# Attention and two feed-forward layers: both products of weights and v of a head pair become one operation, the last block of keys gets 128 rows, and the order of the operations is another

## The chip, the cores and the metric

The kernel runs on one core of a Trainium2 chip. The metric is the device time of one execution in microseconds. TensorE (PE) multiplies, VectorE (DVE), ScalarE (ACT) and GpSimd (POOL) do the elementwise work, and SyncE (SP) issues the DMAs.

## The reference, cut to what matters

```python
batch, n_heads, seq, head_dim = (4, 8, 576, 64)
scores = q @ k.T / sqrt(64)
mask = (pos[:, None] // 64) >= (pos[None, :] // 64)     # block-causal, blocks of 64
attn = softmax(where(mask, scores, -1e9))
x = (attn @ v) as [4 * 576 tokens, 512]
x = ((x @ w1) * (x @ w2)) @ w3 @ w_out                  # 512 -> 1024 -> 1024 -> 512
out = elu(x @ w_in) @ w_out2                            # 512 -> 2048 -> 512
```

## The kernel before

The 32 heads are handled as 16 head pairs, two heads of 64 columns side by side. One call of `attention(n, ...)` records the work of pair n: the scores of four groups of 128 queries (`group`, `first_groups`; L641, L648, L715) and of a last block of 64 queries (`last_block`; L780, L786), row maxima on VectorE, exponentials on ScalarE, transposes of the weights on TensorE (L687, L760, L820, L829) into PSUM tiles `t`, copies of them into the SBUF tiles `pt` (a helper at L518 on ScalarE or L519 on VectorE), and the products of weights and v (`pv`, L850) into PSUM tiles `o`, which the same helper copies into `xy`. The sums of the exponentials go out to memory, come back broadcast as `rr`, and `norm` multiplies `xy` by them.

Weights stand transposed in three tiles: `pts[0]` for queries 0 to 255, `pts[1]` for queries 256 to 575 and keys 0 to 511, and `pts[2]` for queries 512 to 575 and the last 64 keys. `pv(0)` multiplies `pts[0]` and v, `pv(1)` multiplies `pts[1]` and `pts[2]` and v. The two heads of a pair take the left and the right half of the array's columns (`o()[D * h:D * h + D, ...]`), so a matmul of L850 stands in the trace as a tile of 128*64, and the one over the last 64 keys as a tile of 64*64. An f32 matmul leaves two records there. All PSUM tiles `t` and `o` of attention take turns on two banks: `turn("to", (3, 4), ...)`.

Beside attention, TensorE has `w_product` (L928: w3 and w_out multiplied into one matrix, 128 records in f32 from the converted tiles `full`), then `block2` (L1042: a and b, L1003: y; 384 columns each) for six tiles of 384 tokens, and then the second feed-forward layer (`part_h`, L1293, and `part_o`, L1372). Weights come as 64-bit words into `cr` and are converted by ScalarE, VectorE and GpSimd before TensorE takes them (L422 to L458).

Nothing runs in the order in which it is written. Every `add` records an operation with its engine, a length and a priority, and `Plan.run` builds one list of them per engine: at each step it takes, of what is ready by its lengths, the one of lowest priority. `TURNS` replaces the priority of single operations by their number, and so sets the order by hand; a matmul of `spare` (L1594) is put in where the plan sees TensorE idle. An engine runs its list strictly in that order.

Of the kernel before, what the change touches and what calls it, by code (L numbers as in the profile page):

```python
# [20 lines left out]
P = 128  # L21
# [264 lines left out]
def attention_moe_moe2(  # L286
# [11 lines left out]
    nc = tc.nc  # L298
    B, NPAIR, _, S = qT.shape
    D = 64  # L300
# [222 lines left out]
    def attention(n, first_op):  # L523
# [36 lines left out]
        for j in range(2):  # L560
            add("SP", 0, lambda j=j: load_v(j), w=[(vt, j)], prio=pr + 2, nbytes=(P * 512 * 4, P * 64 * 4)[j])
# [275 lines left out]
        def pv(c, seq):  # L837
# [18 lines left out]
            if c:  # L856
                r += [(pt, "q"), pts[2], (vt, 1)]
# [794 lines left out]
```

## Time and profile before

| | us |
|---|---|
| median of 3 runs (895.3 to 899.37) | 895.55 |
| the profiled execution | 893.4 |
| span of its trace | 891.3 |
| TensorE busy, share of the span | 98% |
| VectorE, ScalarE, GpSimd busy | 80%, 57%, 61% |

The span runs from the first to the last instruction; the profiled execution is 2.1 us longer than it. Times below are from the span's start.

### The profile page before, as it was taken

What the parts mean: (1) busy time and instruction counts of PE and PEld (TensorE: products, weight loads), DVE (VectorE), ACT (ScalarE), POOL (GpSimd) and SP (SyncE); (2) the same over time, 40 slices, a digit from 0 to 9 for tenths busy, and PEclk for the clock granted to TensorE, in tenths of its full rate; (3) what the DMA queues carried; (4) which work ended last, traced back from release to release, by engine and by line L of the source; (5) the groups of instructions that cost most, each with busy time, mean ns of one, the idle gap of its engine ahead of it and who ended that gap; (6) DMA issues with size and microseconds to landing.
All of it is one profiled execution on the core that took longest, in us unless ns stands there. A gap on an engine that the chain in (4) does not pass through costs nothing.

```text
span 891.3 us, 15293 instructions
## 1 busy us (share of the span) xinstructions
PE 875.9 (98%) x5233; PEld 783.3 (88%) x5233; DVE 717.4 (80%) x1375; ACT 504.0 (57%) x1143; POOL 546.1 (61%) x552
## 2 busy tenths in 40 slices
PE   7999999999999999999999999999999999999998
PEld 4554488888788889999999999999999999999997
DVE  6998898888666666757888899888997779886886
ACT  7877678666655654326354554455644556454461
POOL 3677778654432315768878893136975268942695
PEclk9999999999999999999999999999999999999999
DMA  7867533555422106767585957777688766888656
GB/s 226 246 197 249 185 138 126 165 183 154 146 68 81 42 14 235 254 232 245 168 271 168 330 189 250 246 257 238 234 301 289 259 243 228 296 272 297 229 176 225
DMA packets 101037, 186.14 MB, mean 209 GB/s; under 512 B 8544, under 2 KB 51040, under 8 KB 100960
## 3 DMA queue, kind: packets, MB, share of 16 engines
q1 hardware_dynamic: 100960, 185.18, 63.0%
q8 instruction: 41, 0.67, 0.3%
q14 instruction: 36, 0.29, 0.1%
HBM read 147.85 MB, written 37.30 MB: 208 GB/s over the span
## 4 chain that ended last, share of the span: by engine, by line
PE 82%; DVE 7%; DMA 4%; ACT 2%; issue 2%; POOL 2%; SPq 1%; POOLq 0%; DVEq 0%; ACTq 0%
PE b L1042 10%; PE a L1042 10%; PE y L1003 10%; PE hx L1293 8%; PE ox L1372 8%; PE oz L1372 6%; PE hy L1293 5%; PE hz L1293 5%; PE oy L1372 5%; PE o L850 3%; PE wps L928 3%; PE t L687 2%; DMA cr<-w3T 2%; PE s L648 2%; DMA cr<-w 1%
## 5 line engine op out<-in xcount | busy, mean ns | idle before, releaser
L1003 PE MATMUL y<-g,slab_lo 128*128 128x384 f32 x576 | 115.6, 339 | 1.2 <-DVE xy L1026 1.0
L1042 PE MATMUL a<-xs,slab_lo 128*128 128x384 f32 x576 | 112.0, 337 | 0.0
L1042 PE MATMUL b<-xs,slab_lo 128*128 128x384 f32 x576 | 111.5, 337 | 0.3 <-DVE af L1059 0.3
L1003 PEld LDWEIGHTS y<-g,slab_lo 128*128 128x128 f32 x576 | 99.4, 188 | 3.8 <-DVE xy L1026 1.8
L1042 PEld LDWEIGHTS b<-xs,slab_lo 128*128 128x128 f32 x576 | 100.2, 188 | 0.6 <-DVE af L1059 0.6
L1042 PEld LDWEIGHTS a<-xs,slab_lo 128*128 128x128 f32 x576 | 100.1, 188 | 0.6 <-issue 0.5
L1293 PE MATMUL hx<-sy,win 128*128 128x384 f32 x432 | 86.4, 334 | 0.0
L1293 PEld LDWEIGHTS hx<-sy,win 128*128 128x128 f32 x432 | 75.8, 188 | 0.1
L1372 PE MATMUL ox<-sp,wout 128*128 128x384 f32 x372 | 74.6, 334 | 0.0
L964 POOL TENSOR_TENSOR g<-af,g 128x384 fp32r<-128x384 f32 x48 | 54.6, 1141 | 29.4 <-ACT g L961 27.2
L1372 PEld LDWEIGHTS ox<-sp,wout 128*128 128x128 f32 x372 | 65.4, 188 | 0.0
L928 PE MATMUL wps<-full,full 128*128 128x512 f32 x128 | 58.5, 597 | 2.9 <-POOL full L452 2.9
L1166 POOL TENSOR_TENSOR sp<-sum,sp 128x384 fp32r<-128x384 f32 x30 | 32.5, 1087 | 45.0 <-ACT sp L1165 45.0
L1293 PE MATMUL hz<-sy,win 128*128 128x384 f32 x288 | 57.9, 335 | 0.2
L1293 PE MATMUL hy<-sy,win 128*128 128x384 f32 x288 | 57.5, 334 | 0.0
L422 ACT ACTIVATE cr<-cr 128x512 int32<-128x512 uint32 x72 | 48.7, 680 | 12.4 <-DMA cr<-w 8.4
L449 POOL TENSOR_TENSOR ct<-ct,cr 128x512 int32<-128x512 int32 x28 | 39.9, 1431 | 22.5 <-DVE ct L443 14.8
L429 ACT ACTIVATE ct<-cr 128x512 f32<-128x512 f32 x58 | 39.4, 678 | 25.1 <-POOL wt L452 15.7
L850 PE MATMUL o<-pt,v 128*64 128x320 f32 (+4 forms) x448 | 52.7, 367 | 0.2
L1372 PE MATMUL oz<-sp,wout 128*128 128x384 f32 x264 | 52.0, 335 | 0.5 <-DVE cp L1175 0.5
L850 PEld LDWEIGHTS o<-pt,v 128*64 128x64 f32 (+1 forms) x448 | 27.8, 135 | 27.6 <-issue 5.5
L1372 PE MATMUL oy<-sp,wout 128*128 128x384 f32 x252 | 51.8, 334 | 0.0
(193 smaller groups left out, 2166.6 us busy)
## 6 DMA issues: line engine op xcount, KB each, us to landing
wout<-wso SPq DMA_DIRECT2D x84, 512.0 KB
cr<-w SPq DMA_DIRECT2D x48, 512.0 KB
win<-wsi SPq DMA_DIRECT2D x24, 1024.0 KB
win<-wsi SPq DMA_DIRECT2D x24, 768.0 KB
cr<-w3T SPq DMA_DIRECT2D x16, 512.0 KB
wsi<-wh SPq DMA_DIRECT2D x8, 896.0 KB
wsi<-wt SPq DMA_DIRECT2D x8, 896.0 KB
wso<-wh SPq DMA_DIRECT2D x8, 896.0 KB
```

Of the source, the lines that this page charges most:

```text
L422: nc.scalar.activation(out=low, in_=low.bitcast(U32), func=AF.Copy, scale=2.0**-29)
L429: nc.scalar.activation(out=t().bitcast(F32), in_=words()[1].bitcast(F32), func=AF.Abs)
L449: nc.gpsimd.tensor_tensor(out=t(), in0=t(), in1=words()[0], op=ALU.add)
L648: nc.tensor.matmul(sb[h]()[:, 0:w], lhsT=qs()[r, a, g * P:(g + 1) * P], rhs=ks()[r, c, 0:w], start=(x == 0), stop=(x == 2 and not added),)
L850: nc.tensor.matmul(o()[D * h:D * h + D, lo:cols], lhsT=vt()[0:kn, j, D * h:D * h + D], rhs=p, start=(j == 0), stop=(j == last),)
L928: nc.tensor.matmul(ps(), lhsT=a[:, j, :], rhs=bb, start=(j == 0), stop=(j == KF - 1))
L964: lambda: nc.gpsimd.tensor_tensor(out=g()[:, 1, :], in0=src(), in1=g()[:, 0, :].bitcast(F32), op=ALU.subtract),
L1003: nc.tensor.matmul(ps()[:, 0:T2], lhsT=w[:, a, n * P:(n + 1) * P], rhs=gs[m]()[:, c, :], start=(m == ms[0] and q == 0), stop=(m == ms[-1] ...
L1042: nc.tensor.matmul(ps()[:, 0:T2], lhsT=w[:, a, u, k, :], rhs=xs()[:, k, c, :], start=(k == 0 and q == 0), stop=(k == KD - 1 and q == 2),)
L1166: lo = lambda eng: eng.tensor_tensor(out=dst(1), in0=src(), in1=dst(0).bitcast(F32), op=ALU.subtract)
L1293: nc.tensor.matmul(bk()[:, 0:T3], lhsT=w[:, a, k, :], rhs=s_(c), start=(first and k == 0 and i == 0), stop=(k == 1 and i == 2), skip_group ...
L1372: nc.tensor.matmul(to[n]()[:, 0:T3], lhsT=w[:, a, n * P:(n + 1) * P], rhs=sp(c), start=(first and q == 0 and i == 0), stop=(q == KP - 1 an ...
```

## The change

`pv` is called once for each head pair, after `last_block`, and records one TensorE operation that multiplies first queries 0 to 255 (four matmuls, into one PSUM tile) and then queries 256 to 575 (ten, into the other); it takes both banks of the turn at once. The last block of keys is made 128 rows long: the transpose at L829 takes keys 448 to 575 and not 512 to 575, v has 64 rows of zeros put in at row 512 by the host, and v's second load takes 128 rows, 64 KB and not 32 KB. So the last two matmuls of a product are tiles of 128*64 like the others. The two copies out of PSUM stay two. `TURNS` is a new table, so the order of all engines is another one.

```diff
 TURNS = {
-    5: -2499.99, 16: -2329.56, 17: -2495.99, 29: -2498.01, 32: -2329.57, 33: -10133.18, 35: -2499.98, 41: -2499.99,
...
+    4: -2500.59, 5: -2499.99, 21: -2498.03, 24: -2399.95, 32: -2399.94, 42: -2500.01, 44: -2518.58, 46: -2499.94,
...
             if j:
-                nc.sync.dma_start(out=vt()[0:64, 4, :], in_=v[b, 512:576, hp * P:(hp + 1) * P])
+                nc.sync.dma_start(out=vt()[:, 4, :], in_=v[b, 512:640, hp * P:(hp + 1) * P])
...
             add(
-                "PE", 0.109, lambda: nc.tensor.transpose(t1()[0:D, 0:P], p()[:, 512:576], ident),
+                "PE", 0.109, lambda: nc.tensor.transpose(t1()[:, 0:P], p()[:, 448:576], ident),
                 r=[(p, 1), "ident"], w=[t1], prio=pg, kind="t",
             )
             evac(
-                128, lambda: pts[2]()[0:D], lambda: t1()[0:D, 0:P].rearrange("p (h q) -> p h q", h=2),
+                128, lambda: pts[2](), lambda: t1()[:, 0:P].rearrange("p (h q) -> p h q", h=2),
                 [t1], [pts[2]], pg,
             )
 
-        def pv(c, seq):
+        def pv(seq):
             pg = pr + 2 + seq
-            pt = pts[c]
-            o = turn("to", (3, 4), "o")
-            q0, cols = ((0, 256), (256, 320))[c]
-            last = (q0 + cols - 1) // P
+            os_ = [turn("to", (3, 4), "o") for _ in range(2)]
+            spans = ((0, 256), (256, 320))
 
             def product():
-                for j in range(last + 1):
-                    lo = max(0, j * P - q0)
-                    kn = min(P, S - j * P)
-                    for h in range(2):
-                        p = pts[2]()[0:kn, h, :] if j == 4 else pt()[:, h, j, lo:cols]
-                        nc.tensor.matmul(
-                            o()[D * h:D * h + D, lo:cols], lhsT=vt()[0:kn, j, D * h:D * h + D],
-                            rhs=p, start=(j == 0), stop=(j == last),
-                        )
-
-            r = [(pt, h, 2 * c + g) for h in range(2) for g in range(2)] + [(vt, 0)]
-            if c:
-                r += [(pt, "q"), pts[2], (vt, 1)]
-            add("PE", (0.8, 2.353)[c], product, r=r, w=[o], prio=pg, kind="pv")
+                for c, (q0, cols) in enumerate(spans):
+                    last = (q0 + cols - 1) // P
+                    for j in range(last + 1):
+                        lo = max(0, j * P - q0)
+                        for h in range(2):
+                            p = pts[2]()[:, h, :] if j == 4 else pts[c]()[:, h, j, lo:cols]
+                            nc.tensor.matmul(
+                                os_[c]()[D * h:D * h + D, lo:cols], lhsT=vt()[:, j, D * h:D * h + D],
+                                rhs=p, start=(j == 0), stop=(j == last),
+                            )
+
+            r = [(pts[g // 2], h, g) for h in range(2) for g in range(4)]
+            r += [(pts[1], "q"), pts[2], (vt, 0), (vt, 1)]
+            add("PE", 2.9, product, r=r, w=os_, prio=pg, kind="pv")
...
         group(2, 2)
-        pv(0, 2.5)
         group(3, 3)
         last_block(4)
-        pv(1, 5)
+        pv(5)
...
-        "vt": lay(v.transpose(0, 2, 1, 3)).reshape(B, S, H * D),
+        "vt": lay(np.insert(v.transpose(0, 2, 1, 3).reshape(B, S, H * D), [512] * 64, 0.0, axis=1)),
```

Two places on TensorE show how the order moves; lines of the changed kernel are a few numbers lower (L850 is L844 there, L829 is L824). The first is the start of the program. Before, the first product of the first head pair (pt_201) stands ahead of the second pair's first scores, and its second product (pt_256) some forty rows behind them:

```order
L687 MATMUL t_268<-ident,p_263 128x128 x4
L780 MATMUL s_275<-k_130,qw 128x288
L850 MATMUL o_284<-pt_201,v_180 64x256 x2
L850 MATMUL o_284<-pt_201,v_180 64x128 x2
L715 MATMUL s_300<-k_247,q_193 128x256
...
L928 MATMUL wps_354<-full_320,full_341 128x512
...
L829 MATMUL t_374<-ident,p_293 64x128
L760 MATMUL t_387<-ident,p_348 128x128
L760 MATMUL t_387<-ident,p_377 128x128
L850 MATMUL o_392<-pt_256,v_180 64x320 x6
L850 MATMUL o_392<-pt_256,v_180 64x192 x2
L850 MATMUL o_392<-pt_381,v_180 64x64 x2
```

In the changed kernel the same place reads:

```order
L775 MATMUL s_279<-k_130,qw 128x288
L682 MATMUL t_284<-ident,p_277 128x128 x4
...
L710 MATMUL s_305<-k_244,q_193 128x256
...
L815 MATMUL t_332<-ident,p_295 128x128 x4
...
L844 MATMUL o_351<-pt_201,v_180 64x256 x2
L844 MATMUL o_351<-pt_201,v_180 64x128 x2
L844 MATMUL o_356<-pt_254,v_180 64x320 x6
L844 MATMUL o_356<-pt_254,v_180 64x192 x2
L844 MATMUL o_356<-pt_341,v_180 64x64 x2
L643 MATMUL s_389<-k_244,q_193 128x384
```

Both products now stand behind the second pair's first scores and ahead of the first `wps` and of that pair's next scores.

The second place is a pair in the middle of attention (before: o_2799 and o_2917; s are scores, t transposes, a and b the block2 matmuls):

```order
L648 MATMUL s_2790<-k_2365,q_2291 128x512
L850 MATMUL o_2799<-pt_2746,v_2495 64x256 x2
L850 MATMUL o_2799<-pt_2746,v_2495 64x128 x2
L687 MATMUL t_2809<-ident,p_2770 128x128 x3
L1042 MATMUL b_2816<-xs_2190,slab_lo_1227 128x384 x12
...
L820 MATMUL t_2886<-ident,p_2873 128x128 x4
L829 MATMUL t_2893<-ident,p_2873 64x128
...
L715 MATMUL s_2897<-k_2607,q_2549 128x256
L850 MATMUL o_2917<-pt_2786,v_2495 64x320 x6
L850 MATMUL o_2917<-pt_2786,v_2495 64x192 x2
L850 MATMUL o_2917<-pt_2914,v_2495 64x64 x2
L648 MATMUL s_2956<-k_2607,q_2549 128x384
```

The same pair in the changed kernel:

```order
L643 MATMUL s_2790<-k_2358,q_2304 128x512
L682 MATMUL t_2801<-ident,p_2774 128x128 x3
L1038 MATMUL a_2808<-xs_2171,slab_lo_1236 128x384 x12
...
L815 MATMUL t_2911<-ident,p_2888 128x128 x4
L824 MATMUL t_2921<-ident,p_2888 128x128
...
L710 MATMUL s_2925<-k_2583,q_2529 128x256
L844 MATMUL o_2948<-pt_2753,v_2473 64x256 x2
L844 MATMUL o_2948<-pt_2753,v_2473 64x128 x2
L844 MATMUL o_2953<-pt_2786,v_2473 64x320 x6
L844 MATMUL o_2953<-pt_2786,v_2473 64x192 x2
L844 MATMUL o_2953<-pt_2941,v_2473 64x64 x2
L643 MATMUL s_2985<-k_2583,q_2529 128x384
```

The first product has left its place between scores and transposes and stands right ahead of the second one.

## Rows read from the trace of the kernel before

**Rows 1.** The page, part 1: busy us, share of the span, instructions.
```profile
PE 875.9 (98%) x5233; PEld 783.3 (88%) x5233; DVE 717.4 (80%) x1375; ACT 504.0 (57%) x1143; POOL 546.1 (61%) x552
```

**Rows 2.** The page, part 4: the chain that ended last, by engine.
```profile
PE 82%; DVE 7%; DMA 4%; ACT 2%; issue 2%; POOL 2%; SPq 1%; POOLq 0%; DVEq 0%; ACTq 0%
```

**Rows 3.** Busy us by stretch (instructions); then granted clock, DMA share, GB/s.
```profile
core 0: us, PE busy (x) PEld busy (x) DVE busy (x) ACT busy (x) POOL busy (x), PEclk, DMA share, GB/s
0.00:112.60 112.60, 104.44 (x507) 54.55 (x509) 97.11 (x197) 84.52 (x196) 72.22 (x90) 1.00 0.71 221
112.60:335.50 222.90, 221.75 (x1578) 183.01 (x1575) 169.92 (x439) 145.08 (x400) 105.63 (x128) 1.00 0.35 111
335.50:891.30 555.80, 549.68 (x3153) 545.75 (x3152) 450.40 (x742) 274.41 (x547) 368.29 (x335) 1.00 0.73 245
```

**Rows 4.** Timeline of PE: start, length, what, [idle before <- releaser].
```profile
121.61 0.87 PE L850 MATMUL o<-pt,v 128*64 128x256 f32 x8
122.41 0.66 PE L687 MATMUL t<-ident,p 128*128 128x128 f32 x4
...
132.58 1.20 PE L1042 MATMUL b<-xs,slab_lo 128*128 128x384 f32 x6
133.62 1.21 PE L1042 MATMUL a<-xs,slab_lo 128*128 128x384 f32 x6
134.76 0.98 PE L715 MATMUL s<-k,q 64*128 64x256 f32 x12
...
138.48 2.42 PE L850 MATMUL o<-pt,v 128*64 128x320 f32 x20
140.83 0.79 PE L648 MATMUL s<-k,q 64*128 64x384 f32 x6
```

**Rows 5.** Timeline of PE in stretches of 0.01 us inside one product.
```profile
138.80 0.44 PE L850 MATMUL o<-pt,v 128*64 128x320 f32 x2
...
139.07 0.44 PE L850 MATMUL o<-pt,v 128*64 128x320 f32 x2
```

**Rows 6.** Timeline of the weight loads (PEld), same stretch as rows 4.
```profile
121.61 0.63 PEld L850 LDWEIGHTS o<-pt,v 128*64 128x64 f32 x8 [0.25 <-issue]
...
136.05 0.11 PEld L829 LDWEIGHTS t<-ident,p 128*64 128x64 f32 x1
136.16 2.06 PEld L1042 LDWEIGHTS a<-xs,slab_lo 128*128 128x128 f32 x12
138.47 1.81 PEld L850 LDWEIGHTS o<-pt,v 128*64 128x64 f32 x16 [0.25 <-ACT ct L429]
140.57 0.20 PEld L850 LDWEIGHTS o<-pt,v 64*64 64x64 f32 x4 [0.28 <-issue]
```

**Rows 7.** Timeline of PE near the start and around 86 us.
```profile
15.04 0.87 PE L850 MATMUL o<-pt,v 128*64 128x256 f32 x8
17.41 0.61 PE L715 MATMUL s<-k,q 64*128 64x256 f32 x6 [1.50 <-ACT p L676]
...
20.84 1.13 PE L928 MATMUL wps<-full,full 128*128 128x512 f32 x2 [1.05 <-POOL full L452]
...
23.56 0.44 PE L760 MATMUL t<-ident,p 128*128 128x128 f32 x2 [0.60 <-DVE pt L519]
...
86.38 5.82 PE L928 MATMUL wps<-full,full 128*128 128x512 f32 x13 [1.55 <-POOL full L452]
```

**Rows 8.** Copies of transposed weights out of PSUM: busy us, mean ns of one.
```profile
L518 ACT COPY pt<-t 128x512 f32<-128x512 f32 x34 | 19.9, 584 | 8.8 <-PE t L820 4.2 <-PE t L760 2.7 <-PE t L687 1.4
...
L519 DVE COPY pt<-t 128x512 f32<-128x512 f32 x30 | 20.6, 686 | 7.8 <-PE t L820 6.5 <-PE t L687 0.6
```

**Rows 9.** DMA issues: how many, KB each.
```profile
v<-vt SPq DMA_DIRECT2D x16, 32.0 KB
```

**Rows 10.** What PE waited for after 335 us: in total, times, longest.
```profile
PE y L1003 <- DVE xy L1026: 1.0, 2, 0.7
PE oy L1372 <- DMA wout<-wso: 0.5, 1, 0.5
```

More of the change, by code (lines that the diff above doesn't have):

```diff
@@ L560, in attention @@
         for j in range(2):
-            add("SP", 0, lambda j=j: load_v(j), w=[(vt, j)], prio=pr + 2, nbytes=(P * 512 * 4, P * 64 * 4)[j])
+            add("SP", 0, lambda j=j: load_v(j), w=[(vt, j)], prio=pr + 2, nbytes=(P * 512 * 4, P * P * 4)[j])
         def f32(x, part):
@@ L855, in pv @@
-            r = [(pt, h, 2 * c + g) for h in range(2) for g in range(2)] + [(vt, 0)]
-            if c:
-                r += [(pt, "q"), pts[2], (vt, 1)]
-            add("PE", (0.8, 2.353)[c], product, r=r, w=[o], prio=pg, kind="pv")
-            x = xy[b]
-            evac(cols, lambda: x()[:, hp, q0:q0 + cols], lambda: o()[:, 0:cols], [o], [(x, hp, c)], pg)
+                for c, (q0, cols) in enumerate(spans):
[8 more added lines that the diff above has]
+                            )
@@ L862, in attention @@
+            r = [(pts[g // 2], h, g) for h in range(2) for g in range(4)]
+            r += [(pts[1], "q"), pts[2], (vt, 0), (vt, 1)]
+            add("PE", 2.9, product, r=r, w=os_, prio=pg, kind="pv")
+            x = xy[b]
+            for c, (q0, cols) in enumerate(spans):
+                evac(
+                    cols, lambda q0=q0, cols=cols: x()[:, hp, q0:q0 + cols], lambda c=c, cols=cols: os_[c]()[:, 0:cols],
+                    [os_[c]], [(x, hp, c)], pg,
+                )
         pts = [r.next() for r in pt_r]
```

121 rows, old and new, of the table TURNS are left out of this document.

## The prediction

> **What bounds the kernel now.** I read the busy shares first: TensorE is busy for 98% of the span [rows 1]. The chain that ended last says the same: 82% of its length is TensorE, and no other engine has over 7% [rows 2]. So a microsecond of TensorE work that is taken away is a microsecond gained, as long as the work behind it is ready. Where that holds is read by stretch [rows 3]. Up to 112.6 us attention's first head pairs, the products `wps` and the conversion of weights run together; TensorE stands idle for 8.2 us of them (112.60 less 104.44), VectorE is busy for 97.1 of 112.6 us, and some of the idle time ends with a converted weight. From 112.6 to 335.5 us the other twelve pairs are mixed with `block2`, and TensorE is idle for only 1.2 us. After 335.5 us it is idle for 6.1 us of 555.8. The clock is granted in full in all three, 1.00 of 2.4 GHz, so no term here comes from the clock.
>
> The reader is then to look at what a product costs [rows 4]. The first one of a pair starts at 121.61 and the next operation at 122.41: 0.80 us. The second one takes from 138.48 to 140.83: 2.35 us. Together that is 3.15 us a pair.
>
> **The change, part by part.**
>
> *The product itself.* Inside it, two neighbouring pairs of records with 320 columns start 0.267 us apart (138.80 and 139.07) [rows 5], 0.834 ns a column. The first product has 256, 256, 128 and 128 columns (heads side by side, two records a head), 768 in all, or 0.64 us; it takes 0.80, so 0.16 us are the way in and the way out. The second has six times 320, twice 192 and twice 64, 2432 columns or 2.03 us, and takes 2.35: over by 0.32. The extra 0.16 has a place: ahead of the loads for the 64*64 tile the weight loader is idle for 0.28 us [rows 6], and the same idle time (0.25) stands ahead of the first load of each product, where the tile changes from 128*128 to 128*64. In the joint product there is one way in and out and no 64*64 tile: 3200 columns are 2.67 us, plus 0.16 is 2.83. The last blocks have 64 columns, so that there the loads could be the limit. Eight loads of 128*64 took 0.63 us [rows 6], 0.08 each; four of them in 0.32 us, where 64 columns twice need 0.11, would make it 3.04. Those loads were paced by matmuls of 128 and 256 columns and so are hardly at their limit; I take 2.85. That saves 0.30 us a pair (bounds 0.11 and 0.32), 4.8 us over sixteen, of which 3.6 belong to the twelve pairs after 112 us and 1.2 to the first four.
>
> *What stands around it.* Six block2 matmuls take 1.04 us (132.58 to 133.62), but 1.14 when scores, on a tile of 64*128, follow them (133.62 to 134.76) [rows 4]: going into a smaller tile costs 0.10. Counted in the two orders of TensorE, leaving L829 out, there are 54 such ways in before and 46 after. It is not sixteen fewer, since a product that stood between two sets of scores cost no way in, and fewer stand so now. Eight times 0.10 is 0.8 us, 0.6 of it late.
>
> *L829.* A transpose of 128*64 becomes one of 128*128. It starts loading at 136.05 and the block2 matmul's load follows at 136.16 with no idle time [rows 6], so I give nothing for it. The Trainium skill, "TensorEngine Tiling (Array Packing)", section Key Properties, says that changing the tiling mode drains TensorE. By that rule each of these transposes costs a drain on its way in and out as well, and the gain would be larger by the second rival's 2.5 us. The rows agree with it for the products and not for L829, so the sum leaves it out.
>
> *Copies and DMA.* The two copies of `o` and the copy of `pts[2]` stay; the columns of the latter do, too. Sixteen loads of v grow from 32 KB [rows 9] to 64 KB, 0.5 MB in all. In the first stretch four of them are 0.13 MB, 0.6 us at its 221 GB/s, with the DMA engines in use for 0.71 of the time [rows 3]; later the share is 0.35. It is hidden in what is free; uncovered it would cost at most 0.6 us, since v is wanted only at the pair's end.
>
> *What is late next.* The product used to fill gaps early. At the start, TensorE ran the first product (15.04), stood idle for 1.50 us until 17.41, and then 1.05 us for a converted weight and 0.60 us for a copy [rows 7]. In the new order all of the pair's product stands ahead of that `wps`. So 0.80 us of work is missing ahead of 17.41, and 2.85 us of it covers the waits of 1.05 and 0.60: a net 0.85 us. With 1.2 and 0.2 us from above, the first four pairs could give 2.25 us. But at 86.38 TensorE waits for 1.55 us for a converted weight [rows 7], and a TensorE that comes earlier would only wait longer there, if conversion is no earlier. Conversion needs slots that earlier `wps` free, so it would follow in part. Between 0 and 2.25 I take 1.1.
>
> Behind the joint product stand the next pair's scores in most pairs, then its transposes, which need the two banks back. The first tile of `o` is finished some 2 us ahead of the product's end, so its copy is covered by the second half; the second tile's copy lies beside scores of about 0.7 us (140.83 on) and the first transposes.
>
> *The rest of the order.* After 335 us the order changes with no work removed. Idle time there is 6.1 us, in single waits of up to 0.7 us (the largest two groups, 1.0 and 0.5 us, in rows 10). A new order moves such waits. I give it 0, with bounds of 3 us either way, half of what there is.
>
> *Sum.* 3.6 + 0.6 + 1.1 = 5.3 us less than the profiled execution's 893.4 us: 888.1. That execution was 2.15 us shorter than the median of the runs, 895.55, so against the median I predict **890.2 us**.
>
> **The rivals.**
>
> *First: all of it comes through.* The early 2.25 us survive, because the freed slots let conversion run earlier, and the late waits halve. 3.6 + 0.6 + 2.25 + 3 = 9.4 us: 886.1. For it speaks that the product is moved into an early gap; against it VectorE's 97.1 us in that stretch. 17%.
>
> *Second: every change of tile shape costs.* The new order has 68 fewer changes of shape, of which 16 are the 64*64 tiles and 25 stand around L829. If those 25 cost 0.10 us each, 2.5 us more are gained: 887.7. The skill's rule above would have it so; the loads at 136.05 and 136.16 [rows 6] speak against it. 5%.
>
> *Third: the freed time is waited away.* Nothing of the early gain passes 86.38, and the new order after 335 us has half as much idle time again, 3 us. 4.2 less 3 leaves 1.2 us: 894.4. The two groups of late waits, for VectorE and a DMA [rows 10], show that such waits arise where one engine's list is a little late, and a TensorE that is 4 us ahead meets more of them. 17%.
>
> *Fourth: slower.* The joint product needs both banks of the turn and all weights of the pair, `pts[1]`'s last 512-column copy among them, while `pv(0)` needed one bank and the weights of two groups. The copy takes 0.58 us on ScalarE and 0.69 on VectorE [rows 8]. If it is late by its whole length in each pair, because ScalarE or VectorE has other work first, TensorE waits at the joint product's first load for 0.69 us sixteen times, 11 us: 895.55 - 5.3 + 11 = 901.3. It decides from 0.33 us a product on (5.3 / 16). Against it: in the order from 0.5 us (three block2 matmuls) to 1.5 us stand between the last transposes and the product, mostly a pair's first scores with 0.9 us. 11%.
>
> **How the numbers follow.** My forecast has 50%, and a range of its own of 887 to 893 (inner bounds of the product, early 0 to 2.25, and some of the late 3). A measurement of this kernel tells about 0.5% from no change, that is 4.5 us: under 891.1 is faster, over 900.0 slower. Faster are 0.34 of the forecast's 0.50, the first two rivals, 0.22, and a little of the third, 0.02: 0.58. Slower is most of the fourth: 0.09. The rest, 0.33, is no change. The range of 885 to 897 leaves out the lower part of the first rival and most of the fourth, together under 2 in 10.
>
> **What the new profile would show.** The product from its first record to the next operation: 2.85 us, no load of 64*64, no idle load inside it; 3.04 would mean that loads are the limit. The way in from block2: still 0.10, and 16 products. L829's successor: its load still 0.11 us behind, with no idle time. The last product's end: about 330 us, where before the second stretch ended at 335.5; if it is there and the whole is not shorter, the loss lies after 335 us, and the idle time of the last stretch, 6.1 us before, tells. At about 86 us: one wait for a converted weight, longer or shorter than 1.55 us. The prediction is wrong if TensorE's idle time in the first stretch grows by over 2 us, if waits ahead of the product pass 0.33 us each, or if the late idle time moves by over 3 us.

## The result and the profile after

The changed kernel takes 887.48 us (median of 4 runs, 886.65 to 888.89), the kernel before beside it 896.45 us (4 runs, 895.30 to 899.37). The ratio is 0.9897, with a 95% interval from 0.9867 to 0.9926: faster, by 9.0 us of the medians. The profiled execution after took 886.9 us, with a span of 885.1. Against the profiled execution before (893.4, span 891.3) that is 6.5 us, 6.2 of them in the span. The forecast was 890.2 us with a range of 885 to 897; its 5.3 us were counted from 895.55, the median of three of these runs of the kernel before.

The first view is part 1 of the page after (busy us, share, instructions), to be laid beside [rows 1].

```profile
PE 872.0 (99%) x5235; PEld 785.7 (89%) x5235; DVE 720.9 (81%) x1361; ACT 511.2 (58%) x1160; POOL 541.6 (61%) x549
```

TensorE still bounds the kernel; it is busy for 3.9 us less. The same three stretches as in [rows 3], cut at the same times, show that the idle time changed mostly at the start: 5.7 us up to 112.6 where it was 8.2, then 1.7 (1.2 before), then 5.6 (6.1 before).

```profile
0.00:112.60 112.60, 106.86 (x521) 56.58 (x522) 100.46 (x203) 87.22 (x205) 70.06 (x90) 1.00 0.71 225
112.60:335.50 222.90, 221.18 (x1599) 189.43 (x1598) 171.09 (x424) 152.32 (x415) 105.36 (x128) 1.00 0.38 120
335.50:885.10 549.60, 543.96 (x3119) 539.70 (x3117) 449.39 (x736) 271.70 (x541) 366.15 (x333) 1.00 0.74 245
```

Cut at fixed times, the stretches hold different work. So I cut both traces at two events: the first `block2` matmul, and the end of the last product. The columns are again length, then busy us (and instructions) of PE, PEld, DVE, ACT, POOL, clock, DMA share, GB/s. First before:

```profile
0.00:114.84 114.84, 106.68 (x518) 55.83 (x518) 99.31 (x201) 86.16 (x199) 73.73 (x91) 1.00 0.70 219
114.84:335.25 220.41, 219.26 (x1566) 181.49 (x1564) 167.59 (x433) 143.44 (x398) 104.12 (x127) 1.00 0.35 111
335.25:891.30 556.05, 549.93 (x3156) 546.00 (x3153) 450.54 (x742) 274.41 (x547) 368.29 (x335) 1.00 0.73 245
```

Then after:

```profile
0.00:112.24 112.24, 106.50 (x519) 56.22 (x520) 100.13 (x202) 86.86 (x204) 69.70 (x90) 1.00 0.71 225
112.24:329.25 217.01, 215.29 (x1564) 183.54 (x1564) 169.43 (x419) 150.95 (x412) 104.44 (x126) 1.00 0.37 115
329.25:885.10 555.85, 550.21 (x3157) 545.95 (x3153) 451.37 (x741) 273.43 (x545) 367.43 (x334) 1.00 0.74 246
```

The three lengths fall by 2.6, 3.4 and 0.2 us: the 6.2 us of the span. In the first stretch it is idle time that goes (8.2 to 5.7), in the second it is busy time (219.3 to 215.3), and the third has the same of both within half a microsecond.

The product itself, in the timeline of PE (start, length, what, idle before), beside [rows 4]: it starts at 144.79 and the next operation at 147.64, so it takes 2.85 us.

```profile
143.65 1.20 PE L1038 MATMUL b<-xs,slab_lo 128*128 128x384 f32 x6
144.79 2.92 PE L844 MATMUL o<-pt,v 128*64 128x256 f32 x28
147.64 0.80 PE L643 MATMUL s<-k,q 64*128 64x384 f32 x6
```

In the timeline of the weight loads, beside [rows 6], the 28 loads are one row with idle time only ahead of the first; the 64*64 loads and the 0.28 us ahead of them are gone. The transpose at L824 (L829 before) is one of 128*128, and its successor's load still follows 0.11 us behind, with no idle time.

```profile
141.84 0.14 PEld L824 LDWEIGHTS t<-ident,p 128*128 128x128 f32 x1
141.95 0.83 PEld L999 LDWEIGHTS y<-g,slab_lo 128*128 128x128 f32 x5
...
144.79 2.79 PEld L844 LDWEIGHTS o<-pt,v 128*64 128x64 f32 x28 [0.25 <-issue]
147.64 0.47 PEld L643 LDWEIGHTS s<-k,q 64*128 64x128 f32 x6
```

Near the start, beside [rows 7]: the second pair's first scores, which waited for 1.50 us, wait for 0.39, the product waits for 0.86 us for a copy, and the wait of 1.55 us at 86.38 is one of 0.49 at 82.10, for the copy of an earlier `wps` into `slab_lo` and no longer for a converted weight.

```profile
16.73 0.61 PE L710 MATMUL s<-k,q 64*128 64x256 f32 x5 [0.39 <-ACT p L804]
...
19.64 2.93 PE L844 MATMUL o<-pt,v 128*64 128x256 f32 x28 [0.86 <-DVE pt L514]
...
25.06 0.87 PE L755 MATMUL t<-ident,p 128*128 128x128 f32 x6 [0.68 <-ACT xy L513]
...
82.10 1.10 PE L924 MATMUL wps<-full,full 128*128 128x512 f32 x2 [0.49 <-DVE slab_lo L938]
...
112.24 1.28 PE L1038 MATMUL a<-xs,slab_lo 128*128 128x384 f32 x6 [0.86 <-DVE ct L438]
```

What PE waited for after 335 us (in total, times, longest), beside [rows 10]: other waits of about the same size.

```profile
PE hz L1289 <- DMA win<-wsi: 1.2, 3, 0.7
PE hz L1289 <- ACT ga L1303: 0.4, 1, 0.4
```

### The profile page after: what moved, and what is told of

Its sections match the earlier page's. It is cut to its first block, busy times and chain, and to the rows that moved or that the text cites. A ratio compares the mean times of both kernels' runs of the same rounds, so it can differ in the third digit from the quotient of the medians.

```text
span 885.1 us, 15302 instructions
## 1 busy us (share of the span) xinstructions
PE 872.0 (99%) x5235; PEld 785.7 (89%) x5235; DVE 720.9 (81%) x1361; ACT 511.2 (58%) x1160; POOL 541.6 (61%) x549
## 4 chain that ended last, share of the span: by engine, by line
PE 83%; DVE 7%; DMA 5%; ACT 2%; issue 1%; SPq 1%; POOL 1%; DVEq 0%; POOLq 0%; ACTq 0%
PE a L1038 11%; PE b L1038 11%; PE y L999 11%; PE ox L1368 8%; PE hx L1289 8%; PE oy L1368 5%; PE oz L1368 5%; PE hy L1289 5%; PE hz L1289 5%; PE o L844 4%; DMA win<-wsi 2%; PE t L682 2%; PE s L643 2%; DMA cr<-w3T 1%; PE t L755 1%
## 5 line engine op out<-in xcount | busy, mean ns | idle before, releaser
L1038 PE MATMUL a<-xs,slab_lo 128*128 128x384 f32 x576 | 110.2, 336 | 0.9 <-DVE ct L438 0.9
L1162 POOL TENSOR_TENSOR sp<-sum,sp 128x384 fp32r<-128x384 f32 x29 | 30.7, 1064 | 39.8 <-ACT sp L1161 39.8
L1289 PEld LDWEIGHTS hz<-sy,win 128*128 128x128 f32 x288 | 50.4, 188 | 2.9 <-DMA win<-wsi 1.5
L1289 PEld LDWEIGHTS hy<-sy,win 128*128 128x128 f32 x288 | 50.4, 188 | 1.1 <-DVE ga L1254 0.7
L1161 ACT CAST sp<-sum 128x384 fp32r<-128x384 f32 x60 | 30.4, 512 | 35.3 <-PE ox L1368 12.8
```

What stands on the lines that cost most here:

```text
L1038: nc.tensor.matmul(ps()[:, 0:T2], lhsT=w[:, a, u, k, :], rhs=xs()[:, k, c, :], start=(k == 0 and q == 0), stop=(k == KD - 1 and q == 2),)
L1161: add("ACT", act_us(n, True), lambda: nc.scalar.copy(dst(0), src()), r=keys, w=[dkeys[0]], prio=prio)
L1162: lo = lambda eng: eng.tensor_tensor(out=dst(1), in0=src(), in1=dst(0).bitcast(F32), op=ALU.subtract)
L1289: nc.tensor.matmul(bk()[:, 0:T3], lhsT=w[:, a, k, :], rhs=s_(c), start=(first and k == 0 and i == 0), stop=(k == 1 and i == 2), skip_group ...
```

## The experiments

Three theories run through them. One is my forecast's: what is gained is the work that TensorE no longer does, and it comes through under any order. The second is that the new order makes the gain, and the joint product little of it. The third is that neither does it alone, since an order fixed in advance fits only the operations for which it was made.

To change one of them without the other, most kernels here don't plan: they read one list of operations with their engines, taken from the plan of before or of after, and emit it row by row. So every engine and every DMA queue gets the order of that list.

```diff
-TURNS = {
...
+TURNS = {}
+SEQ = (
...
     def run(self):
...
+        for n, e in re.findall(r"(\d+)([A-Z])", SEQ):
...
+            o = self.ops[int(n)]
...
+            o.eng = names[e]
+            o.us, o.fn, _ = o.ways[o.eng]
             o.fn()
```

| experiment | product | order | us (median, range, runs) | before beside it | ratio, 95% interval |
|---|---|---|---|---|---|
| e4 | joint, 128 rows | new | 887.39 (886.04 to 888.62, 6) | 895.54 | 0.9905 [0.9890, 0.9921] |
| e1 | joint, 64 rows | new | 887.48 (886.16 to 887.85, 6) | 895.54 | 0.9907 [0.9891, 0.9923] |
| e2 | joint, 128 rows | old | 911.03 (909.33 to 914.18, 5) | 895.54 | 1.0175 [1.0154, 1.0196] |
| e3 | two, 128 rows | new | 899.31 (898.36 to 900.22, 6) | 895.54 | 1.0041 [1.0026, 1.0056] |
| e5 | two, 64 rows | planned without `TURNS` | 909.06 (908.19 to 910.40, 6) | 896.37 | 1.0138 [1.0113, 1.0163] |
| e6 | joint, 128 rows | planned without `TURNS` | 903.12 (902.09 to 905.46, 6) | 896.37 | 1.0077 [1.0049, 1.0105] |
| e7 | joint, 128 rows | planned with old `TURNS` | 909.03 (905.38 to 911.56, 6) | 896.37 | 1.0134 [1.0102, 1.0166] |
| e8 | joint, 128 rows | new, old at the end | 887.05 (886.27 to 889.43, 6) | 896.37 | 0.9898 [0.9872, 0.9923] |
| e9 | two, 128 rows | old | 895.51 (893.22 to 898.45, 12) | 896.42 | 0.9992 [0.9976, 1.0008] |
| e10 | joint, 64 rows | planned without `TURNS` | 905.09 (902.44 to 906.53, 6) | 896.42 | 1.0100 [1.0076, 1.0123] |
| e11 | joint, 128 rows | new, old for a part | 889.23 (886.49 to 890.56, 6) | 896.42 | 0.9919 [0.9893, 0.9944] |

**e4, the changed kernel from its own list.** The edit is the one above.

> The changed kernel once more, the same order of every engine, written out as a list: 887.5 us by either theory, and its span tells how far two executions of one order lie apart (the four runs so far: spans of 884.9 to 887.1 us).

It gives the changed kernel's time again, so the list is what matters, and the others can be compared with it.

**e1, the last block back to 64 rows, in the new order.**

```diff
-                nc.sync.dma_start(out=vt()[:, 4, :], in_=v[b, 512:640, hp * P:(hp + 1) * P])
+                nc.sync.dma_start(out=vt()[0:64, 4, :], in_=v[b, 576:640, hp * P:(hp + 1) * P])
...
-                "PE", 0.109, lambda: nc.tensor.transpose(t1()[:, 0:P], p()[:, 448:576], ident),
+                "PE", 0.109, lambda: nc.tensor.transpose(t1()[0:D, 0:P], p()[:, 512:576], ident),
...
+                        kn = 64 if j == 4 else P
...
-                                os_[c]()[D * h:D * h + D, lo:cols], lhsT=vt()[:, j, D * h:D * h + D],
+                                os_[c]()[D * h:D * h + D, lo:cols], lhsT=vt()[0:kn, j, D * h:D * h + D],
```

> The changed kernel with every engine's order kept row by row, and only the last block of keys taken back to 64 rows (transpose of 64x128, v's second load of 32 KB, last two matmuls of a product on a tile of 64*64). Theory A (each product is paid for by its columns, one way in and out, and a drain at the 64*64 tile): the product takes 2.96 us and not 2.855, 16 x 0.10 = 1.6 us slower than the changed kernel, about 889 us. Theory B (the gain is the new order's, and time freed in a product is waited away): no change, 887.5 us. Rule that every change of tile shape drains, L829's transposes too: 2.5 us more than A.

The weight loads of e1 show the idle 0.28 us ahead of the 64*64 loads again, and the product takes 3.00 us (143.91 to 146.91).

```profile
143.91 2.46 PEld L976 LDWEIGHTS o<-pt,v 128*64 128x64 f32 x24 [0.25 <-issue]
146.65 0.20 PEld L976 LDWEIGHTS o<-pt,v 64*64 64x64 f32 x4 [0.28 <-issue]
146.91 0.47 PEld L774 LDWEIGHTS s<-k,q 64*128 64x128 f32 x6
```

Sixteen times 0.15 us are 2.4 us of work, and the time is the same to 0.1 us. Cut at the same two events, the stretches of e1 are 0.9 shorter, 1.0 longer (twelve products make 1.8) and 0.5 shorter: part of the work shows where it is done, and waits elsewhere fell away. So in the order that was made for the wide block, the narrow one costs nothing that the runs can tell.

**e2, the joint product in the old order.** The list is that of before, with a pair's first product moved to where the second stood. In four pairs the joint product stands earlier than that, ahead of the next pair's first transposes, which need its bank.

```diff
-        pv(0, 2.5)
...
         last_block(4)
-        pv(1, 5)
+        pv(5)
```

> The kernel before with its old order of every engine, in which only the first product of each pair is moved to the second one (the joint product of 128 rows; it stands a row or two earlier where the next transposes need its bank). Theory A: sixteen products at 0.30 us less and a few ways in at 0.10: 4.8 to 6 us less than before, about 891 us, and the last product ends some 5 us earlier than in the kernel before. Theory B: the time is waited away in the old order, within 1.5 us of before, 895 us. Fourth rival of the prediction (waits for both banks): slower than before.

It is 15.5 us slower than before, although the product takes 2.85 us here too. TensorE's idle time grows by 14.8 us, from 15.4 to 30.2. The longest of what PE waited for up to 350 us:

```profile
PE t L819 <- DVE pt L651: 3.4, 4, 1.2
PE t L892 <- DVE xy L651: 3.2, 3, 1.9
PE s L847 <- ACT p L808: 2.3, 1, 2.3
PE s L780 <- ACT p L808: 2.3, 3, 1.4
```

The copies of weights (`pt`), of `o` (`xy`) and the exponentials (`p`) come too late for the operations behind them. A place in the timeline of e2, in one of the middle pairs:

```profile
178.13 0.65 PE L819 MATMUL t<-ident,p 128*128 128x128 f32 x4 [1.19 <-DVE pt L651]
...
188.48 0.66 PE L952 MATMUL t<-ident,p 128*128 128x128 f32 x4 [0.79 <-DVE pt L651]
189.81 2.92 PE L981 MATMUL o<-pt,v 128*64 128x256 f32 x28 [0.68 <-ACT pt L650]
```

Before, the first product, 0.80 us, stood among these operations; that it gave the copies their time is read from the order, and no run put other work of that length there. The last of the three rows is the wait that the fourth rival named, of the size that it gave: 0.68 us at the product, for `pts`. It is there at two of the sixteen products (0.78 us at the other), and both are among the four that stand earlier, without the pair's first scores between the transposes and the product. So e2 is not quite the old order, and a part of its loss belongs to these places.

**e3, two products in the new order.** The first stands ahead of the transposes of its pair's fourth group of queries, the second where the joint one stands; both have the wide block.

```diff
-        def pv(seq):
+        def pv(c, seq):
...
-            add("PE", 2.9, product, r=r, w=os_, prio=pg, kind="pv")
+            add("PE", (0.8, 2.353)[c], product, r=r, w=[o], prio=pg, kind="pv")
```

> The changed kernel with its new order of every engine and the wide last block, but the first product of each pair on its own again, ahead of the transposes of the fourth group of queries, its copy right behind it. Theory A: 0.20 us a pair inside the products (3.05 and not 2.855) and a way in of 0.10: about 4.8 us more than the changed kernel, 892 us. Theory B: within 1.5 us of the changed kernel, 888 us.

It is 11.9 us above e4. The second product takes 2.20 us (150.04 to 152.24), so both together 3.00, and 0.15 us over the joint one makes 2.4 us of the 11.9. In the traces TensorE is busy for 5.6 us more than in e4 and idle for 8.1 us more. So most of the loss is waits; which row causes them, and whether another place for the first product would cost less, was not tried.

```profile
150.04 2.27 PE L983 MATMUL o<-pt,v 128*64 128x320 f32 x20
152.24 0.79 PE L781 MATMUL s<-k,q 64*128 64x384 f32 x6
```

e2 and e3 together bear the third theory out: each half of the change, put by itself into an order made for something else, makes the kernel slower than before.

**e5, e6 and e7, the planner's own orders.** e5 is the kernel before and e6 the changed one, both with `TURNS` empty, so that the rules alone order the work; e7 is the changed kernel with the numbers of before, carried over to the operations' new numbers.

```diff
 TURNS = {
-    4: -2500.59, 5: -2499.99, 21: -2498.03, 24: -2399.95, 32: -2399.94, 42: -2500.01, 44: -2518.58, 46: -2499.94,
...
 }
```

> The kernel before with an empty table of turns: every operation keeps its own priority and the plan makes the order by its rules alone. It is the partner of the next kernel. Slower than the kernel before by what the table was worth, 5 to 20 us (900 to 915 us).

> The changed kernel with an empty table of turns, planned by the same rules as the kernel with separate products and an empty table. Theory A (the work saved is gained once each kernel has an order planned for it): 4 to 6 us less than that one. Theory C (the joint product loses as much in waits as it saves in work, and only the search for a new table made it good): within 2 us of it or slower.

> The joint product with the old table of turns carried over operation by operation, and the order planned anew around it. Before, the old order taken as it stood cost 911 us. Theory A: planning finds other work for the gaps that the first product filled, so most of the 15 us are gone, 890 to 900 us. Theory C: it stays near 905 to 911 us, since the table was found for separate products.

Under the same rules the joint product is worth 5.9 us (909.06 to 903.12), near the 4.8 us of work plus the ways in that the forecast counted over sixteen pairs. On the pages TensorE's busy time falls from 881.6 to 876.5 us. So the joint product's work does come through where the order is made for it. This is one pair of orders; how far two orders of the planner lie apart by chance was not tried.

With the old numbers the joint product is 12.7 us slower than before and gains nothing on e5. The numbers, worth 12.7 us to the kernel before (909.06 to 896.37), are not worth it here. Part of e7's loss is TensorE's clock. The first of these rows of e7 is the stretch ahead of the longest fall, the second the fall itself (length, PE busy, granted clock, DMA):

```profile
207.60:217.80 10.20, 7.05 (x53) 1.00 0.73 216
217.80:228.00 10.20, 8.31 (x44) 0.50 0.40 137
```

The granted clock is 0.50, the lower of its two levels (1.2 and not 2.4 GHz), in three stretches of e7, 17 us together, and the product in the one above takes 5.52 us and not 2.85. TensorE was idle for 3.2 of the 10.2 us before it fell. It is busy for 15.2 of the 17 us; at the full clock that work would take half as long, so an estimate from these rows is 7.6 us. The waits of the order came first and the slower clock was added to them. How much of the 12.7 us would be left at the full clock, no run shows. (e5 has one such stretch of 3.4 us, and e6 and e10 one of 6.8 each, so the clock did not make the 5.9 us; after their start before, after, e1 to e4, e8, e9 and e11 have none.)

**e9 and e10, the wide block by itself.** e9 is before's list with the last block widened, e10 is e6 with the narrow block.

```diff
-                nc.sync.dma_start(out=vt()[0:64, 4, :], in_=v[b, 512:576, hp * P:(hp + 1) * P])
+                nc.sync.dma_start(out=vt()[:, 4, :], in_=v[b, 512:640, hp * P:(hp + 1) * P])
...
-                    kn = min(P, S - j * P)
+                    kn = P
```

> The kernel before with every engine's order kept row by row and both products apart, and only the last block of keys made 128 rows long. The second product takes 2.205 us and not 2.353 (seen where the products were put apart in the new order), 16 x 0.15 = 2.4 us of TensorE work less. Theory A (work saved is time gained): about 893 us, ratio 0.9973. Theory D (in an order found for another length, what a product is shorter is waited for behind it): within 1 us of before, as the last block of 64 rows cost the changed kernel no time.

> The joint product with an empty table of turns (903.1 us) with the last block back at 64 rows and the same order: products of 3.00 us and not 2.855. Theory A: 2.4 us more, 905.5 us. Theory D: the same 903 us.

The wide block takes 0.15 us from e9's second product (2.20 for 2.35), 2.4 us in all. The medians show 0.9 us, with an interval from 2.2 us less to 0.7 us more. In e9's trace the gain can be seen where it is made: between the first `block2` matmul and the end of the last product, the stretch is 2.1 us shorter than before and busy for 1.6 us less (twelve products make 1.8).

```profile
116.25:334.56 218.31, 217.61 (x1565) 182.89 (x1564) 166.82 (x433) 143.21 (x398) 104.67 (x127) 1.00 0.36 113
```

The start of that execution is 1.4 us longer (116.25 for 114.84), for a reason told in the last section, and so its span is the same 891 us. e10 is 2.0 us above e6, in runs beside other runs of the kernel before, and their intervals overlap. With e1's 0.1 us, the widening is worth something from nothing to 2.4 us of the kernel's time; more the runs don't settle.

**e8 and e11, the old order late.** e8 has the new order up to about the 1,950th matmul of 384 columns (some 567 us) and the old one behind it; e11 has the old one only between the 1,950th and the 3,480th. Only rows of the list differ from e4's; e8's first one that does:

```diff
 SEQ = (
...
-    "2924O 2911P 2777D 2794S 2778P 2932O 2913D 2920P 2779D 2783P 2780D 2781A 2908P 2782D 2912P 2784D 2928A 2921P "
+    "2924O 2908P 2777D 2794S 2911P 2932O 2928A 2778P 2913D 2929O 2912P 2779D 2941O 2920P 2914D 2933A 2940S 2783P "
...
```

> The changed kernel in its own order up to some 1950 block2 and later matmuls (about 567 us), and from there what is left in the old order. In the two traces the changed kernel was 8.0 us ahead of the old one there and 6.2 at the end, so that the old order's end should give 1.8 us: 885.6 us. If waits follow from what came before and not from the order at that place, it stays at 887.4 us.

> The changed kernel's order, the old order between some 1950 and 3480 block2 and later matmuls, and the changed kernel's order for the end. The old order's middle was 1.3 us ahead of the changed kernel at 3500 matmuls in the kernel of two parts, which lost it again to a DMA at the end. If that end was the only loss: 886 us; the interval can hardly tell it from 887.4, so the trace's marks decide.

Neither beats the changed kernel beyond its interval. In e8 the 3,500th of these matmuls, counted over the trace, starts at 837.1 us, where it starts at 838.4 after; then TensorE waits twice, 0.45 us for VectorE and 0.85 us for a transfer of `w_out2`, and the lead is gone. The second wait:

```profile
865.80 2.25 PE L1499 MATMUL ox<-sp,wout 128*128 128x384 f32 x12
868.89 2.36 PE L1499 MATMUL oy<-sp,wout 128*128 128x384 f32 x12 [0.85 <-DMA wout<-wso]
```

e11 was to take the lead and keep after's end. Its profiled execution was already 1.8 us late at the first `block2` matmul, in rows that are the same in both lists (last section). Counted from that matmul, the 3,500th starts 326.1 us later in e11, 326.2 after and 324.5 in e8, and the rest takes 48.3, 46.7 and 48.4 us. So the old order's middle did not bring its lead along, and the end was not kept either.

## Why the prediction was right, and where it was off

*The product.* Taken at 2.85 us, it takes 2.85 in all sixteen pairs; 0.30 us a pair is what it saves. The loads are not the limit at the last blocks, since that would have made it 3.04. The parts are apart, too: 0.15 us is the 64*64 tile (e1, e9), and 0.15 the second way in and out.

*The second stretch.* 3.6 us for twelve products and 0.6 for fewer ways into smaller tiles make 4.2; busy time fell by 4.0 between the same two events. The length fell by 3.4, since TensorE was idle for 0.6 us more: a little of the third rival.

*L829.* Nothing was given for it, and the second rival would have made the gain 2.5 us larger. Its successor's load still follows 0.11 us behind, as in [rows 6], and with 4.0 us of busy time where 4.2 were forecast without it, there is no room for that. The Trainium skill, "TensorEngine Tiling (Array Packing)", section Key Properties, has it that a change of the tiling mode drains TensorE: the idle 0.28 us ahead of the 64*64 loads agree, L829 does not.

*The early stretch: the step that was off.* The forecast said that 2.25 us of gain could arise in the first four pairs, and that half would be lost at 86.38, waiting longer for a converted weight. It was 2.6 us, and from another source. Busy time fell by only 0.2 us, not by 1.4, and idle time by 2.4. The four products do take 1.2 us less; among what took it up are 13 matmuls of `spare` for 11, which are put in where the plan sees TensorE idle. Up to the first `block2` matmul these waits of PE stood in before's trace:

```profile
PE wps L928 <- POOL full L452: 2.9, 3, 1.5
PE spare L1594 <- POOL mk L1440: 2.0, 1, 2.0
PE s L715 <- ACT p L676: 1.5, 1, 1.5
PE t L760 <- DVE pt L519: 0.6, 1, 0.6
PE t L687 <- ACT xy L518: 0.5, 1, 0.5
PE t L687 <- ACT p L676: 0.5, 1, 0.5
```

and these in the trace after:

```profile
PE spare L1590 <- POOL mk L1436: 2.0, 1, 2.0
PE a L1038 <- DVE ct L438: 0.9, 1, 0.9
PE o L844 <- DVE pt L514: 0.9, 1, 0.9
PE t L755 <- ACT xy L513: 0.7, 1, 0.7
PE wps L924 <- DVE slab_lo L938: 0.5, 1, 0.5
PE s L710 <- ACT p L804: 0.4, 1, 0.4
```

The waits of `wps` for converted weights, 2.9 us, are gone, the scores' wait is 1.1 us shorter, and three waits of transposes, 1.6 us, are gone; four new ones take 3.0 us of that back. I had taken the conversion as fixed and asked only how early TensorE would come to it. The new order has the converted weights there in time for `wps`, though not for the first `block2` matmul: its weight load waits until `slab_lo` is written by the conversion, and 0.9 us of that is TensorE's.

```profile
PEld a L1038 <- ACT slab_lo L479: 1.7, 1, 1.7
```

Which moved row of VectorE, ScalarE or GpSimd did that was not tried by itself.

*The late order.* Taken at nothing, with 3 us either way. The third stretch is 0.2 us shorter, with 5.6 us of idle time for 6.1. The waits of [rows 10] are gone, and three for `win` have come.

*The sum.* 5.3 us were forecast against the profiled execution and 6.5 measured: 1.5 more early, 0.8 less in the second stretch, 0.2 more in the third, and 0.3 outside the span. So the errors of two stretches offset each other in part, which is luck. The medians differ by 9.0, and 887.48 lies nearer the first rival's 886.1 and the second's 887.7 than 890.2. The traces bear neither out: of the first rival the early half came (2.6 us for its 2.25), the late 3 us did not (0.2), and of the second nothing is seen at L829. In all runs here the kernel before took from 893.1 to 900.5 us, the changed one from 886.0 to 888.9; before's profiled execution, with 893.4, is one of its shortest. The other 2.5 us of the medians are such differences between executions. What before's longer ones lose, and why the changed kernel varies less, no trace here shows; the start told of in the last section is one candidate.

*The fourth rival* named a wait at the joint product, 0.69 us in each pair. With the new order it is there up to 350 us in one row, for 0.86 us (L844 above), and in e2 at two products. Most of what made e2 slow is beside it: waits at transposes and scores, for copies and exponentials ahead of which the first product no longer stands. I had weighed only what stands ahead of the product, and not that the copies ahead of it lose 0.80 us of cover; in the new order few such waits are left (at most 1.1 us up to 350 us, the start's 2.0 for `mk` aside), and the forecast has no term for either.

What stays open: how the last 3 us of the medians divide between product and order, which row brought the converted weights earlier, and why e1's 2.4 us of work are not seen in its time.

## What to carry to other kernels

Where one engine is busy for 98% of the span, the work of a merged operation can be priced to a hundredth of a microsecond from columns and the idle time ahead of its loads, and in these runs that price came through only where the order was made anew: the short operation that is merged away may have been what covered a copy. So such a change is better judged with both versions under the same planning rules (here 5.9 us) than by putting it into an order tuned for the old one (here 15.5 us the wrong way). Before two traces are compared by stretch, look at the granted clock and at the first matmuls of each: here both differed between kernels without the change being the cause. Before saying that an earlier engine will only wait longer, ask whether the new order also moves what it waits for.

## What the runs showed of the hardware

Executions of one list differ by 2 us (e1) to 7 us (the kernel before), and some 2 us can arise in the first 14 us. These are the first pair's scores in the groups of PE by line (busy us, mean ns of one), after and then in e11, which has the same list up to some 567 us:

```profile
L636 PE MATMUL s<-k,q 64*128 64x512 f32 x4 | 1.9, 641 | 0.0
```

```profile
L767 PE MATMUL s<-k,q 64*128 64x512 f32 x4 | 2.1, 1138 | 0.0
```

The same matmuls take 1.8 times as long in e11. They do in e9, too (1075 ns). The cause is TensorE's clock, although the granted clock reads 1.00 in these windows. Within e11 the same transposes change their speed. Here are four of them from 10.3 us on, and four from 13.9 us on:

```profile
L813 PE MATMUL t<-ident,p 128*128 128x128 f32 x4 | 1.1, 431 | 0.0
L813 PE MATMUL t<-ident,p 128*128 128x128 f32 x4 | 0.7, 304 | 0.0
```

They start 0.213 us apart at 11 us and 0.110 us apart at 14.2 us, a factor of 1.94, and after has the 0.110 at 9.3 us already. The trace's own records of the clock begin at 14.05 us in e11, just where the speed changes, and at 5.31 us after; a stretch without a record reads as 1.00. So TensorE started at the lower of its two levels, 1.2 GHz, in both, and rose 8.7 us later in e11. The first record stands at 14.15 us in e9, 13.49 in e10, 10.95 in e2, and between 5.2 and 6.4 in the others; for before it is 6.34, so that the 1.00 of [rows 3] says nothing of its first 6 us either. The first `block2` matmul came at 114.0 us in e11 and at 112.2 after, and 1.4 us later in e9 than before. Up to about 5 us TensorE had done the same operations at the same times in e11 and after; why its clock rose later in e11, no row tells.
